# A gated SSM and MLP block: the first token tile turned by TensorE in place of a DMA transpose, and the last output piece 64 columns wide

## The chip, the cores and the metric

The kernel runs on one core of a Trainium2 chip. The metric is the device time of one execution in microseconds, as the median of several runs. Matmuls run on TensorE (PE in the profile, its weight loads are PEld), elementwise work on VectorE (DVE) and ScalarE (ACT), small set-up on GpSimd (POOL). DMAs are issued from SyncE's queue (SP) and from ScalarE's queue (ACTq).

## The reference

One input x of 2048 tokens by 640 features (bf16) goes through two branches, and a gate mixes them:

```python
g = sigmoid((x * gate_w).sum(-1, keepdims=True))
# branch A: a diagonal complex state space model with 640 states, scanned over the 2048 tokens
Lam_bar = exp(dt * Lam)
h_t = Lam_bar * h_(t-1) + B_bar @ x_t
a = 2 * real(C @ h) + x * Dskip
# branch B: an MLP, 640 -> 1728 -> 640
b = gelu(x @ w1 + b1) @ w2 + b2
out = g * a + (1 - g) * b
```

## The kernel before

**Tiling.** Tokens are worked in four chunks of 512 (CH), each of four token tiles of 128 (TPC = 4). Features are worked in five blocks of 128 (KD = 5). TensorE needs x with features on the partitions; that form is `xT[c]`, one tile of 128 x 5 x 512 for each chunk. `xn[c]` is x as it lies in memory, tokens on the partitions; branch A's skip term reads it later (`seed`, L577 to L584).

**Stages.** For each chunk: `ff1` (first MLP layer, L305), `ssm` (the B matmuls and the scan on DVE, L541), `fin_b` (second MLP layer, L606), `fin_a` (the C matmuls, the gate and the output, L654). The lines from L687 to L711 set the order of these stages by hand; the order of instructions on TensorE, DVE and ACT is the order in which the program names them, except that DVE work put off by `later` is let out by a small planner with written-down costs (`Clock`, L195). The planner's numbers are not fed by the operations that the change touches at the start.

**The start of chunk 0.** Six PSUM banks hold the first six blocks of 128 columns of the first MLP layer (FA = 6). They are filled strip by strip: strip kd is feature block kd, with weights `w1a[kd]` (128 x 768, 192 KB), and within a strip `part(kd, a)` (L356) does the six matmuls of 128 columns for token tile a. This way TensorE can begin when one token tile and one weight strip are there. Nine matmuls on a constant, up to 512 columns wide (L233), and three more (L359) run before them and have no result that is used: fillers.

How x of chunk 0 is turned:
- token tile 0, feature blocks 0 and 1 (KA = 2): by one DMA transpose straight into `xT[0]`, first on SP's queue (L140);
- token tiles 1 to 3, feature blocks 0 and 1: loaded into `xn[0]` by `load_x0` and turned by TensorE in `turn_first` (L248): two matmuls against an identity, into two PSUM tiles, then one copy to bf16 on DVE (L244) and one on ACT (L246);
- feature blocks 2 to 4 of all four tiles: loaded as `load_x0(…, KA * P, D)` and turned by `turn_rest` (L331).

The order on TensorE is: nine fillers; three fillers; part(0,0); turn_first(1); part(1,0); turn_first(2); part(0,1); part(1,1); turn_first(3); part(0,2); part(1,2); the small matmul that turns the parameters (L370); turn_rest(0); and so on.

**DMA queues.** At the head of SP's queue stand the transpose of tile 0, x of tile 2, x of tile 3, `w1a[2]`. At the head of ACT's queue stand `w1a[0]`, x of tile 1, `w1a[1]`, the rest of x for tiles 0 and 1. After them SP's queue has the parameters, the rest of x for tiles 2 and 3, the last weights strips of `w1a` (L156), `w1b` in five DMAs (L160), `w1c` in four DMAs (two strips together in the tile `w1c34`, L161, then three), the transposes of B, x and C, `w2`, and then a plain load of tile 0's first 256 features into `xn[0]` (L185), since the transpose at the head does not fill it.

Eight semaphores count the landings, in turn over both queues: each DMA takes the semaphore of the DMA eight places earlier, and its queue waits until that one has landed before it issues.

The DVE copies at L400 put one column with the gate's weights behind the 448 loaded columns of each `w1c[j]`.

**The end.** Output rows are written one token tile at a time. `cuts` (L574) says in which column pieces a tile is made: two of 320, and three for the very last tile (NT - 1). For each piece `fin_a` does ten matmuls, then DVE combines (L673). For the last tile, the first two pieces leave by one store from SP's queue (L680) and the last by a store from ACT's queue.

Of the kernel before, what the change touches and what calls it, by code (L numbers as in the profile page):

```python
# [12 lines left out]
BF16 = mybir.dt.bfloat16  # L13
# [3 lines left out]
P = 128  # L17
T = 2048
D = 640
F = 1728  # L20
CH = 512
NCH = T // CH
KD = D // P
# [3 lines left out]
NT = T // P  # L27
# [4 lines left out]
HD = D // 2  # L32
# [9 lines left out]
def kernel(  # L42
# [19 lines left out]
    nc = tc.nc  # L62
    x2d = A_x.flatten_outer_dims()
# [3 lines left out]
    const = ctx.enter_context(tc.tile_pool(name="const", bufs=1))  # L67
# [7 lines left out]
    def bank(dtype=F32):  # L75
        return ps.tile([P, CH * 4 // (4 if dtype == F32 else 2)], dtype, name="bank")
# [4 lines left out]
    cut2 = FB * P  # L81
    n1c = F - cut2 + 1
    xT = [const.tile([P, KD, CH], BF16, name=f"xT{c}") for c in range(NCH)]
# [1 line left out]
    w1a34 = const.tile([P, 2, cut1], BF16, name="w1a34")  # L85
    w1a += [w1a34[:, j, :] for j in range(2)]
    w1b = [const.tile([P, cut2 - cut1], BF16, name=f"w1b_{kd}") for kd in range(KD)]
    w1c = [const.tile([P, n1c], BF16, name=f"w1c_{kd}") for kd in range(3)]
    w1c34 = const.tile([P, 2, n1c], BF16, name="w1c34")
    w1c += [w1c34[:, j, :] for j in range(2)]  # L90
    w2_sb = const.tile([P, KF - 1, D], BF16, name="w2_sb")
    BT_re, BT_im = ([const.tile([P, KD, n * P], BF16, name=f"BT_{ri}{n}") for n in (KSA, KS - KSA)] for ri in ("re", "im"))
    CT_re = const.tile([P, KS, D], BF16, name="CT_re")
# [34 lines left out]
    def load_w1a(queue, kd):  # L128
        queue.dma_start(out=w1a[kd][:], in_=B_w1[kd * P:(kd + 1) * P, 0:cut1])  # L129
# [4 lines left out]
    KA = 2  # L134
    xn[0] = xnp.tile([P, TPC, D], BF16, name="xn")

    def load_x0(queue, a0, a1, d0, d1):
        queue.dma_start(out=xn[0][:, a0:a1, d0:d1], in_=x2d[a0 * P:a1 * P, d0:d1].rearrange("(a p) d -> p a d", p=P))  # L138

    nc.sync.dma_start_transpose(out=xT[0][:, 0:KA, 0:P], in_=x2d[0:P, 0:KA * P])  # L140
    load_w1a(nc.scalar, 0)
    load_x0(nc.scalar, 1, 2, 0, KA * P)
    load_w1a(nc.scalar, 1)
    load_x0(nc.sync, 2, 3, 0, KA * P)
    load_x0(nc.scalar, 0, H, KA * P, D)
# [12 lines left out]
    rows(nc.sync, prmB[0:KS, :], gate_w)  # L158
    for kd in range(KD):
        nc.sync.dma_start(out=w1b[kd][:], in_=B_w1[kd * P:(kd + 1) * P, cut1:cut2])  # L160
    nc.sync.dma_start(out=w1c34[:, :, 0:F - cut2], in_=B_w1[3 * P:KD * P, cut2:F].rearrange("(k p) f -> p k f", p=P))  # L161
    for kd in range(3):
        nc.sync.dma_start(out=w1c[kd][:, 0:F - cut2], in_=B_w1[kd * P:(kd + 1) * P, cut2:F])
    make_identity(nc, ident[:])
    HC = CH // 8
# [16 lines left out]
        nc.sync.dma_start(out=w2_sb[:, k0:k1, :], in_=B_w2[k0 * P:k1 * P, :].rearrange("(kf p) d -> p kf d", p=P))  # L182
    for h in range(2):
        nc.sync.dma_start(out=w2l[h * F_LAST:(h + 1) * F_LAST, :], in_=B_w2[(KF - 1) * P:F, :])
    load_x0(nc.sync, 0, 1, 0, KA * P)  # L185
    nc.sync.dma_start(out=b2bc[:], in_=B_b2.rearrange("(o d) -> o d", o=1).to_broadcast([P, D]))
    nc.sync.dma_start(out=Dbc[:], in_=A_Dskip.rearrange("(o d) -> o d", o=1).to_broadcast([P, D]))
    nc.sync.dma_start_transpose(out=xT[2][:], in_=x2d[2 * CH:3 * CH, :])
# [43 lines left out]
    pA = bank()  # L232
# [3 lines left out]
    def turn(p, col, a, kd):  # L236
        nc.tensor.matmul(p[:, col:col + P], lhsT=xn[0][:, a, kd * P:(kd + 1) * P], rhs=ident[:], start=True, stop=True,  # L237
                         skip_group_check=True)

    def turned(engine, p, col, a, k0, k1):  # L240
        dst = xT[0][:, k0:k1, a * P:(a + 1) * P]
        src = p[:, col:col + (k1 - k0) * P].rearrange("p (k t) -> p k t", t=P)
        if engine is nc.vector:
            nc.vector.tensor_copy(out=dst, in_=src)  # L244
        else:
            nc.scalar.activation(out=dst, in_=src, func=ACT.Identity)  # L246

    def turn_first(a, other):  # L248
        t = bank()
        turn(t, 0, a, 0)  # L250
        turned(nc.vector, t, 0, a, 0, 1)
        turn(other, a * P, a, 1)
        turned(nc.scalar, other, a * P, a, 1, 2)

    def col(name, dtype=F32, n=KS):
        return const.tile([P, n], dtype, name=name)
# [102 lines left out]
    for _ in range(3):  # L359
        nc.tensor.matmul(banks[0][:, 0:P], lhsT=ones(P), rhs=ones(P), start=True, stop=True, skip_group_check=True)  # L360
    part(0, 0)
    turn_first(1, pA)
    part(1, 0)
    turn_first(2, pA)
    part(0, 1)
    part(1, 1)
    turn_first(3, pA)
    part(0, 2)
    part(1, 2)
# [201 lines left out]
    HALVES = ((0, HD), (HD, D))  # L571
    seeded = {}

    def cuts(ti):  # L574
        return ((0, HD), (HD, 512), (512, D)) if ti == NT - 1 else HALVES

    def seed(ti):  # L577

        c, a = divmod(ti, TPC)
        seeded[ti] = []  # L580
        for d0, d1 in cuts(ti):
            p = bank()
            dve_now(ck.pe, 0.45, lambda: nc.vector.tensor_tensor(out=p[:, 0:d1 - d0], in0=xn[c][:, a, d0:d1], in1=Dbc[:, d0:d1], op=ALU.mult))  # L583
            seeded[ti].append(p)  # L584
# [69 lines left out]
    def fin_a(c, at={}):  # L654
        let_out(0, c)
        for a in range(TPC):
            ti = c * TPC + a
            lo = a * P
            ot = fwork.tile([P, D], BF16, name="ot", bufs=2)
            if a < TPC - 2:  # L660
                seed(ti + 2)
            if a in at:
                at[a]()
            for i, (d0, d1) in enumerate(cuts(ti)):
                p = seeded[ti][i]
                for j in range(2 * KS):
                    CT = CT_re if j < KS else CT_im
                    nc.tensor.matmul(p[:, 0:d1 - d0], lhsT=hs[c][:, j, lo:lo + P], rhs=CT[:, j % KS, d0:d1],  # L668
                                     start=False, stop=(j == 2 * KS - 1), skip_group_check=True)
                    pe(d1 - d0)  # L670

                def f():
                    nc.vector.scalar_tensor_tensor(out=ot[:, d0:d1], in0=p[:, 0:d1 - d0], scalar=gcol[:, 0, ti:ti + 1],  # L673
                                                   in1=gbs[ti][:, d0:d1], op0=ALU.mult, op1=ALU.add)

                dve_now(ck.pe + 0.2, 0.45, f)
                if ti == NT - 1 and i > 0:
                    s0 = 0 if i == 1 else d0
                    q = nc.sync if i == 1 else nc.scalar
                    q.dma_start(out=out2d[ti * P:(ti + 1) * P, s0:d1], in_=ot[:, s0:d1])  # L680
            if ti < NT - 1:
                nc.sync.dma_start(out=out2d[ti * P:(ti + 1) * P, :], in_=ot[:])
# [59 lines left out]
```

## Time and profile before

| what | us |
|---|---|
| median of 3 runs | 217.73 (217.61 to 218.08) |
| the profiled execution | 217.61 |
| its span, first to last instruction | 215.8 |
| TensorE busy | 211.0 (98%) |
| DVE busy | 188.7 (87%) |
| ACT busy | 102.7 (48%) |
| first matmul with x (L269) | at 3.92 |
| second weight strip's first matmul | at 5.47 |
| clock record of TensorE at full rate begins | at 9.16 |
| last combine on DVE begins | at 213.09 |

All times of the profile are counted from the span's start. The execution's own time is 1.81 us longer than its span. A group's count follows an x; an idle time in brackets says how long the engine sat before the group and what released it. "SPq" and "ACTq" lines are the time in which a queue issues a DMA, not the time in which its data move; landings are read from the trace's record of semaphore increments.

### The profile page before, as it was taken

To read this page: it belongs to the slowest core of one execution; us is meant where nothing else is said; L and a number is where in the kernel's file an instruction comes from. 1 tells how busy PE (TensorE), PEld (TensorE's weight loads), DVE (VectorE), ACT (ScalarE), POOL (GpSimd) and SP (SyncE) were. 2 spreads that over 40 slices of the span, in tenths; PEclk is the share of its full clock that TensorE was granted. 3 is DMA by queue.
4 is the path that set the end of the run, shared out by engine and by line. 5 is a ranking of instruction groups with operands and counts; after the bars stand their busy time and mean duration, and the time that the engine had idled before them with its cause. 6 is when DMAs were issued, how large, how long until landed. Compare 5 with 4: busy or idle time off the path is not lost.

```text
span 215.8 us, 3582 instructions
## 1 busy us (share of the span) xinstructions
PE 211.0 (98%) x1397; PEld 128.1 (59%) x1408; DVE 188.7 (87%) x386; ACT 102.7 (48%) x185; POOL 1.0 (0%) x13
## 2 busy tenths in 40 slices
PE   7999999999999999999999999999999999999994
PEld 4964544454466744675457777544456677676773
DVE  1379999999998999999999999999999999994153
ACT  3299956675668579402581310356683421404200
POOL 1000000000000000000000000000000000000000
PEclk9999999999999999999999999999999999999999
DMA  6799999994000000024000002500000000210011
GB/s 157 210 220 191 219 220 318 267 224 138 0 0 0 3 0 2 12 65 151 30 0 3 0 0 42 204 0 2 3 0 14 0 3 9 72 44 0 0 65 61
DMA packets 31843, 15.91 MB, mean 74 GB/s; under 512 B 23250, under 2 KB 31826, under 8 KB 31826
## 3 DMA queue, kind: packets, MB, share of 16 engines
q1 hardware_dynamic: 30978, 14.99, 28.2%
q10 hardware_dynamic: 848, 0.69, 1.3%
q8 instruction: 11, 0.18, 0.4%
q14 instruction: 6, 0.05, 0.1%
HBM read 7.48 MB, written 2.62 MB: 47 GB/s over the span
## 4 chain that ended last, share of the span: by engine, by line
PE 96%; DMA 2%; ACTq 0%; issue 0%; DVE 0%
PE bank L269 27%; PE bank L609 26%; PE bank L668 20%; PE bank L550 20%; DMA w1a<-in_B_w_dram 2%; PE bank L625 1%; PE bank L295 1%; PE bank L237 1%; ACTq L138 0%; ACTq L129 0%; DVE ot L673 0%; PE bank L285 0%; PE bank L370 0%; PE bank L397 0%
## 5 line engine op out<-in xcount | busy, mean ns | idle before, releaser
L609 PE MATMUL bank<-w_sb,gel 128*128 128x384 bf16 (+1 forms) x416 | 57.9, 299 | 0.0
L609 PEld LDWEIGHTS <-gel 128*128 128x128 bf16 x416 | 40.3, 98 | 17.0 <-issue 0.8
L553 ACT ACTIVATE bu<-bank 128x512 bf16<-128x512 f32 x40 | 23.6, 598 | 37.6 <-PE bank L550 37.6
L274 ACT ACTIVATE gel<-bank,colB 128x512 bf16<-128x512 f32 x52 | 33.7, 693 | 10.6 <-PE bank L269 10.4
L668 PEld LDWEIGHTS <-hs 128*128 128x128 bf16 x330 | 31.7, 98 | 11.6
L504 DVE TENSOR_TENSOR_SCAN g<-r_c,carry,v 128x512 bf16<-128x512 f32 x30 | 37.2, 1269 | 0.0
L617 ACT ACTIVATE gb<-bank,gcol 128x384 f32<-128x384 f32 (+1 forms) x32 | 15.1, 525 | 32.7 <-PE bank L609 16.4
L269 PE MATMUL bank<-xT,w1a 128*128 128x512 bf16 (+2 forms) x173 | 29.6, 328 | 0.9 <-DMA w1a<-in_B_w_dram 0.5
L668 PE MATMUL bank<-CT_re,hs 128*128 128x320 bf16 (+2 forms) x165 | 27.1, 295 | 0.0
L668 PE MATMUL bank<-CT_im,hs 128*128 128x320 bf16 (+2 forms) x165 | 27.1, 295 | 0.0
L673 DVE SCALAR_TENSOR_TENSOR ot<-bank,gcol,gb 128x320 bf16<-128x320 f32 (+2 forms) x33 | 17.4, 533 | 9.8 <-PE bank L668 9.5
L550 PE MATMUL bank<-xT,BT_im 128*128 128x512 bf16 x99 | 24.8, 379 | 0.1
L550 PE MATMUL bank<-xT,BT_re 128*128 128x512 bf16 x97 | 24.5, 379 | 0.2
L269 PEld LDWEIGHTS <-w1a 128*128 128x128 bf16 x177 | 16.2, 108 | 12.4 <-DMA w1a<-in_B_w_dram 0.8
L269 PE MATMUL bank<-xT,w1b 128*128 128x512 bf16 x80 | 17.9, 379 | 0.0
L550 PEld LDWEIGHTS <-BT_im 128*128 128x128 bf16 x100 | 9.8, 98 | 11.8
L550 PEld LDWEIGHTS <-BT_re 128*128 128x128 bf16 x100 | 9.7, 98 | 11.0
L583 DVE TENSOR_TENSOR bank<-xn,Dbc 128x320 f32<-128x320 bf16 (+2 forms) x33 | 14.5, 482 | 1.9 <-ACT gb L617 1.9
L485 DVE TENSOR_TENSOR v<-wa,wb 128x512 bf16<-128x512 bf16 x40 | 15.2, 421 | 0.6
L598 ACT ACTIVATE bank<-b2bc 128x384 f32<-128x384 bf16 (+1 forms) x24 | 11.7, 524 | 7.8 <-DVE ot L673 7.8
L485 DVE TENSOR_TENSOR wa<-TCOS,g 128x1024 bf16<-128x1024 bf16 x20 | 13.7, 685 | 0.1
L269 PE MATMUL bank<-xT,w1c 128*128 128x512 bf16 x57 | 13.6, 379 | 0.2
(99 smaller groups left out, 165.8 us busy)
## 6 DMA issues: line engine op xcount, KB each, us to landing
out_dram<-ot SPq DMA_DIRECT2D x15, 160.0 KB, 1.8
w_sb<-in_B_w_dram SPq DMA_DIRECT2D x1, 2080.0 KB
xn<-in_A_x_dram SPq DMA_DIRECT2D x3, 640.0 KB
w1b<-in_B_w_dram SPq DMA_DIRECT2D x5, 128.0 KB, 3.1
w1a<-in_B_w_dram ACTq DMA_DIRECT2D x2, 192.0 KB
w1a<-in_B_w_dram SPq DMA_DIRECT2D x1, 384.0 KB, 3.5
w1c<-in_B_w_dram SPq DMA_DIRECT2D x3, 112.0 KB, 4.3
w1c<-in_B_w_dram SPq DMA_DIRECT2D x1, 224.0 KB, 4.0
```

Source lines behind the costliest of these rows:

```text
L269: nc.tensor.matmul(p[:, t0:t1], lhsT=w, rhs=xT[c][:, kd, t0:t1], start=(kd == 0) if first is None else first, stop=(kd == last), skip_grou ...
L274: nc.scalar.activation(out=gel[c][:, kf, :], in_=p[:, :], func=ACT.Gelu_apprx_tanh, bias=b1_c[:, kf:kf + 1])
L485: nc.vector.tensor_tensor(out=o, in0=a, in1=b, op=op)
L504: nc.vector.tensor_tensor_scan(s["g"][:, ri, :], r_c[:, ks:ks + 1].to_broadcast([P, CH]), s["v"][:, ri, :], init, ALU.mult, ALU.add)
L550: nc.tensor.matmul(p[:], lhsT=BT[ks >= KSA][:, kd, (ks % KSA if ks < KSA else ks - KSA) * P:][:, 0:P], rhs=xT[c][:, kd, :], start=(kd == 0 ...
L553: nc.scalar.activation(out=bu[:, ri, :], in_=p[:], func=ACT.Identity)
L583: dve_now(ck.pe, 0.45, lambda: nc.vector.tensor_tensor(out=p[:, 0:d1 - d0], in0=xn[c][:, a, d0:d1], in1=Dbc[:, d0:d1], op=ALU.mult))
L598: nc.scalar.activation(out=v, in_=src, func=ACT.Identity)
L609: nc.tensor.matmul(p[:, col:col + d1 - d0], lhsT=gel[c][:, kf, a * P:(a + 1) * P], rhs=w2_sb[:, kf, d0:d1], start=False, stop=False, skip_ ...
L617: nc.scalar.activation(out=gbs[ti][:, d0:d1], in_=p[:, col:col + d1 - d0], func=ACT.Identity, scale=gcol[:, 1, ti:ti + 1])
L668: nc.tensor.matmul(p[:, 0:d1 - d0], lhsT=hs[c][:, j, lo:lo + P], rhs=CT[:, j % KS, d0:d1], start=False, stop=(j == 2 * KS - 1), skip_group ...
L673: nc.vector.scalar_tensor_tensor(out=ot[:, d0:d1], in0=p[:, 0:d1 - d0], scalar=gcol[:, 0, ti:ti + 1], in1=gbs[ti][:, d0:d1], op0=ALU.mult, ...
```

## The change

- The DMA transpose at the head of SP's queue becomes a plain load of the same 128 x 256 block into `xn[0]`, and the later load of the block (L185) goes.
- Tile 1's load moves from ACT's queue, where it stood between `w1a[0]` and `w1a[1]`, to SP's queue, where it comes second.
- `turn_first(0, pA)` is added: TensorE turns tile 0's two blocks between the nine fillers and the three fillers, with one copy on DVE and one on ACT.
- `w1c` is five tiles with a DMA each, in place of three and a double one.
- The last tile's pieces are 320, 256 and 64 columns in place of 320, 192 and 128.

Everything else keeps its order on TensorE, DVE and ACT.

```diff
-    w1c = [const.tile([P, n1c], BF16, name=f"w1c_{kd}") for kd in range(3)]
-    w1c34 = const.tile([P, 2, n1c], BF16, name="w1c34")
-    w1c += [w1c34[:, j, :] for j in range(2)]
+    w1c = [const.tile([P, n1c], BF16, name=f"w1c_{kd}") for kd in range(KD)]
...
-    nc.sync.dma_start_transpose(out=xT[0][:, 0:KA, 0:P], in_=x2d[0:P, 0:KA * P])
+    load_x0(nc.sync, 0, 1, 0, KA * P)
     load_w1a(nc.scalar, 0)
-    load_x0(nc.scalar, 1, 2, 0, KA * P)
+    load_x0(nc.sync, 1, 2, 0, KA * P)
     load_w1a(nc.scalar, 1)
     load_x0(nc.sync, 2, 3, 0, KA * P)
...
-    nc.sync.dma_start(out=w1c34[:, :, 0:F - cut2], in_=B_w1[3 * P:KD * P, cut2:F].rearrange("(k p) f -> p k f", p=P))
-    for kd in range(3):
+    for kd in range(KD):
         nc.sync.dma_start(out=w1c[kd][:, 0:F - cut2], in_=B_w1[kd * P:(kd + 1) * P, cut2:F])
...
-    load_x0(nc.sync, 0, 1, 0, KA * P)
...
         turned(nc.scalar, other, a * P, a, 1, 2)
 
+    turn_first(0, pA)
+
...
     def cuts(ti):
-        return ((0, HD), (HD, 512), (512, D)) if ti == NT - 1 else HALVES
+        return ((0, HD), (HD, D - P // 2), (D - P // 2, D)) if ti == NT - 1 else HALVES
```

## The prediction

> **What bounds the kernel now.** I read the page first (busy shares and the clock row), then the chain that ended last, then the timeline of the first six and last five microseconds, and last the busy time by stretch. The page:
>
> ```profile
> PE 211.0 (98%) x1397; PEld 128.1 (59%) x1408; DVE 188.7 (87%) x386; ACT 102.7 (48%) x185; POOL 1.0 (0%) x13
> ```
>
> TensorE is busy all the time, so only its first work, its pace and what follows its last matmul can move the end. The chain, in order of time:
>
> ```profile
> 1.59 0.03 issue
> 1.62 3.81 DMA w1a<-in_B_w_dram
> 5.43 0.05 issue
> 5.47 0.82 PE bank L269 x6
> ...
> 9.28 0.01 PE bank L370
> ...
> 202.16 10.91 PE bank L668 x90
> 213.06 0.03 issue
> 213.09 0.35 DVE ot L673
> ```
>
> The one transfer on it is the second weight strip, w1a_1: third DMA on ACT's queue, issued at 1.62, landed at 5.43. After 5.47 nothing but TensorE until the last `ot`. The timeline of TensorE there, and of the end:
>
> ```profile
> 3.28 0.53 PE L360 MATMUL bank<-const-bfloat16-1.0 128*128 128x128 bf16 x3
> 3.92 0.80 PE L269 MATMUL bank<-xT,w1a 128*128 128x128 bf16 x6
> 4.51 0.42 PE L237 MATMUL bank<-ident,xn 128*128 128x128 bf16 x2
> 5.47 0.82 PE L269 MATMUL bank<-xT,w1a 128*128 128x128 bf16 x6 [0.54 <-DMA w1a<-in_B_w_dram]
> ```
> ```profile
> 212.53 0.91 DVE L673 SCALAR_TENSOR_TENSOR ot<-bank,gcol,gb 128x192 bf16<-128x192 f32 x2 [0.27 <-PE bank L668]
> 212.60 0.44 PE L668 MATMUL bank<-CT_im,hs 128*128 128x128 bf16 x5
> 212.97 0.33 SPq L680 DMA_DIRECT2D out_dram<-ot  x1
> 213.47 0.36 ACTq L680 DMA_DIRECT2D out_dram<-ot  x1
> ```
>
> Two holes: 3.60 (3.495, start of the last filler, plus 0.107) to 3.92, for the DMA transpose (it lands at 3.88 by its semaphore), and 4.73 to 5.47, for w1a_1. The pace, by stretch (first to last us, length, then busy time and count on PE, PEld, DVE, ACT, POOL, clock, DMA share and GB/s):
>
> ```profile
> 5.47:9.16 3.69, 3.69 (x36) 3.69 (x37) 0.58 (x2) 0.55 (x2) 0.00 (x0) 1.00 0.68 196
> 9.16:14.00 4.84, 4.79 (x64) 4.00 (x63) 3.49 (x14) 4.06 (x9) 0.00 (x0) 1.00 0.90 251
> ```
>
> 36 matmuls of 128 columns take 3.69 us before 9.16, 0.107 apart; after it they are 0.056 apart. The clock record starts at 9.164, 3.69 us after the restart at 5.47. So what ends TensorE's last hole sets both the start and the moment of full pace.
>
> **What the skill says.** "TensorE: Matmul & The Clock Gate", Part 1: the array runs at half rate until about 3.4 us of sustained work; the window runs free, so the moment varies; starts are 107 ns apart cold and 56 ns warm at 128 columns. The trace agrees on both paces, and on one rise 3.69 us after a hole; that its moment varies no run here shows. "DMA: Bandwidth & Descriptors", "Issuing engines are not separate DMA queues": SP's and ACT's DMAs share the same 16 engines. "Queues, rings and completion order": a ring is consumed in order, and rings alternate by packet. The trace fits: x1, issued 0.48 after w1a_0 on one queue, lands 0.54 after it (3.67 against 3.13).
>
> **The start, step by step.** Removed: the transpose at SP's head (issue 1.29) and x1 between w1a_0 and w1a_1 on ACT (issue 1.14 to 1.59, with its gap 0.485). Added: a plain 64 KB load of x0 at SP's head, x1 second there; two turns on TensorE, one DVE and one ACT cast.
>
> 1. x0 lands. Nearest rows: x1 took 2.53 from issue, w1a_0 2.40. Issued at 0.73: 3.2 (2.9 if it is quicker without a ring ahead of it, 3.7 if both first issues slow each other).
> 2. Turns: the nine fillers end at 3.28. Two turns of 0.107 from 3.28 to 3.5; the three fillers (0.32) follow to 3.82. Turn to cast is 0.35 (4.515 to 4.866), the DVE cast 0.29, release 0.04: strip block 0 starts at 3.97 against 3.92, +0.05 (0 to +0.5 with a late x0). The hole before it shrinks to 0.15. ACT's new cast (0.28) comes after the table load, which moves from 2.79 to about 2.3 with one issue less; done at about 4.1, before its reader at 4.8.
> 3. The block's six matmuls (0.64) and tile 1's turns (0.21) end at 4.82. x1, issued at about 1.3 on SP, by its 2.53 lands at 3.8: in time.
> 4. w1a_1 is issued at 1.14, not 1.62. If it keeps its 3.80 it lands at 4.94 and TensorE restarts at 4.98: -0.49. If, with nothing between it and w1a_0 in its ring and no transpose beside it, it takes 3.6 or less, it is there at 4.82 and the hole is gone. Worst: the 192 KB move no faster for being asked for earlier, 5.43, gain nil. The bytes ahead of it are the same (x0 for the transpose, x1 in the other ring). I take 4.94.
> 5. With the restart 0.49 earlier and the rise still 3.69 behind it, the rise is at 8.67 and everything after shifts by 0.49. If the hole goes, the last hole ends at 3.97, the rise comes at 7.66, and the sum is larger: 34.6 cold slots ran from 5.47 to 9.16; from 4.82, 26.5 fit until 7.66, the other 8 take 8x0.056=0.45: 8.11 against 9.16, -1.05.
>
> Supply stays ahead. SP's later issues each wait for the landing eight DMAs back: x tiles 2 and 3's rest, now waiting on w1a_1, goes at 5.0 in place of 5.97, w1a's last strips at about 5.4 in place of 6.43. Their slack was 1.7 and 1.5 us (landed 8.40 and 9.96, needed at 10.10 and 11.48). Tightest is x2: needed 0.51 after the restart (5.49), issued some 0.25 earlier, so landed at about 5.4; slack 0.1 where it was 0.33. If that cover goes, the cost is the lateness itself.
>
> **w1c in five DMAs and x0's second load gone.** One issue more (0.43 on SP, median 3 rows) and one less later (0.58). w1c is needed from 18.6; its last piece landed at 15.8. B's transposes behind it had 4.6 us or more (19.0 against 23.64). The DVE copies into w1c's last columns no longer wait for that DMA: 0.33 of DVE idle at 13.8 to 14.1 goes; the weight load at 14.49 that waits on them had 0.16 of slack, so this cover gets better, and the path gets nothing. Zero.
>
> **Later slack.** Where matmuls of the output wait on DVE, the smallest margins are 1.25 (at 176.24) and 1.19 (181.68). A shift up to 1.2 reaches the end whole even if DVE did not move; DVE itself starts from TensorE's early matmul (colA at 9.35), so it moves along.
>
> **The tail.** The last tile is cut 320, 256, 64 in place of 320, 192, 128. TensorE: 10x0.0825+10x0.056=1.38 before; 256 columns are 0.109 apart (strip rows at 11.5), 65 columns 0.61/20=0.0305: 1.09+0.31=1.40, +0.01. DVE: 0.551, 0.418, 0.351 at 320, 192, 128 columns, about 1.04 ns a column: 0.485 and 0.285. The 256 piece starts at 212.79 and ends at 213.28; the 64 piece is ready at 213.10 but queues behind it, ends near 213.50 (213.44 before). ACT's store then lands 1.50 later, 215.03 against 214.97. SP's store goes at 213.30 in place of 212.97 and with its 1.72 plus 0.03 for wider rows lands at 215.05. So SP's store becomes last: +0.08 (0 to +0.2; short rows of 128 bytes are not in the trace).
>
> **Sum.** -0.49 + 0.08 = -0.41: span 215.4, and the profiled execution's 217.61 (span plus 1.81) goes to 217.2. The median shown, 217.73, is 0.12 above that execution: 217.32, say 217.3.
>
> **Rivals.**
> A. The hole at w1a_1 closes (step 4's lower end). For it: w1a_1's packets start near 3.1, after a lull, and would now follow w1a_0's at once. Against: its 16 landings spread over 1.2 us. -1.05+0.08: 216.8.
> B. Early clock: the 0.15 us hole does not count and 3.69 runs from 0.77: the rise by 4.5 to 5.8, up to -1.9, of which DVE's margin may clip some: 215.9 to 216.5. Against: 0.32 of idle was enough to prevent it before.
> C. Nothing gained: w1a_1 lands at 5.4 as before, or x0 comes at 3.7 or later so that blocks 0 and 1 follow each other with no earlier end; tail +0.08: 217.7 to 217.8.
> D. Slower: the clock. If the window runs free, the 3.69 was luck and can be up to 6.8. Each us of later rise costs 0.48 (half pace). With the restart at 4.98 half of the start's gain stays (0.52x0.49=0.25); slower by more than 0.2% needs 0.44+0.25-0.08=0.61 from the clock: a rise 1.3 later than before, past 10.4. For it: the three times spread by 0.47. Against: all three lie close above the lowest. Time 218.2 to 218.6.
>
> **Chances.** Forecast 0.38, A 0.25, B 0.07, C 0.12, D 0.18. 0.2% (0.44 us) is about what a measurement here can tell from none; the forecast stands on that edge, so I give half of it to each side: faster 0.25+0.07+0.19=0.51, same 0.19+0.12=0.31, slower 0.18. The range holds the forecast, A, C and the near half of D: 216.6 to 218.3, some 0.84. The forecast's own range is 217.1 to 217.5.
>
> **What would show it.** Restart of strip 1's block at about 4.98 (A: 4.82 with no hole; C: 5.4 or later); clock record starting at 8.7 (A 7.7, B below 6, D past 10.4); w1a_1 landing 3.8 after an issue at 1.14; block 0 at 3.97; the weight load at w1b not waiting; SP's last store landing after ACT's, some 2.2 us after the last matmul's start. Wrong it would be if x0 lands after 3.7, if the clock's rise is not tied to the last hole, or if some store or weight strip is late.

## The result and the profile after

The changed kernel takes 216.12 us (median of 6 runs, 215.99 to 216.24); the kernel before, run beside it, 217.84 (217.21 to 218.08, 6 runs). The ratio is 0.9924, 95% interval 0.991 to 0.9938. The forecast was 217.3, its range 216.6 to 218.3: the direction was right, the gain was four times the one forecast, and the time lies below the range. The profiled execution took 215.99 with a span of 214.2; before, 217.61 and 215.8.

The page's busy times after:

```profile
PE 209.9 (98%) x1399; PEld 127.1 (59%) x1410; DVE 188.9 (88%) x387; ACT 103.2 (48%) x186; POOL 1.0 (0%) x13
```

TensorE has two matmuls more and yet 1.1 us less of busy time: it ran fewer of them at half pace. The chain that ended last, in order of time (start, length, what):

```profile
0.77 2.72 PE bank L230 x9
3.49 0.21 PE bank L233 x2
3.70 0.32 PE bank L358 x3
4.02 0.75 PE bank L267 x6
4.77 0.21 PE bank L233 x2
4.99 0.64 PE bank L267 x6
...
200.31 10.62 PE bank L666 x80
210.93 0.02 issue
210.95 0.48 DVE ot L671
211.44 0.19 DVEq L735
```

No DMA is left on it. The timeline of TensorE in those microseconds:

```profile
3.28 0.42 PE L233 MATMUL bank<-ident,xn 128*128 128x128 bf16 x2
3.50 0.52 PE L358 MATMUL bank<-const-bfloat16-1.0 128*128 128x128 bf16 x3
3.97 0.80 PE L267 MATMUL bank<-xT,w1a 128*128 128x128 bf16 x6
4.57 0.42 PE L233 MATMUL bank<-ident,xn 128*128 128x128 bf16 x2
4.78 0.84 PE L267 MATMUL bank<-xT,w1a 128*128 128x128 bf16 x6
```

Block 0 starts at 3.97 and strip 1's block at 4.78, with nothing idle ahead of it: w1a_1, issued at 1.16, has landed at 4.19. The hole of 0.74 is gone. The pace, by stretch (first to last us, length, busy time and count on PE, PEld, DVE, ACT, POOL, granted clock, DMA share, GB/s):

```profile
4.00:6.00 2.00, 2.00 (x21) 2.00 (x20) 0.52 (x2) 0.41 (x3) 0.00 (x0) 1.00 0.79 232
6.00:9.00 3.00, 3.00 (x56) 2.99 (x54) 1.73 (x8) 1.39 (x6) 0.00 (x0) 1.00 0.89 272
```

21 matmuls in 2 us, then 56 in 3: the pace nearly doubles at about 6.0. The clock record begins at 6.03; before it began at 9.16. The tail (the two last DVE combines stand in one group):

```profile
210.95 0.68 DVE L671 SCALAR_TENSOR_TENSOR ot<-bank,gcol,gb 128x256 bf16<-128x256 f32 x2 [0.54 <-PE bank L666]
211.47 0.33 SPq L678 DMA_DIRECT2D out_dram<-ot  x1
211.66 0.36 ACTq L678 DMA_DIRECT2D out_dram<-ot  x1
```

**Where the 1.6 us between the two profiled executions went.** Strip 1's block starts 0.69 earlier (4.78 against 5.47). The clock: before, 34.5 matmuls of 0.107 fill the 3.69 us up to the rise at 9.16; after, 11.7 of them fit between 4.78 and 6.03 and the other 22.8 take 0.056 each, 1.28 us. The same work is done at 7.31 in place of 9.16, 1.85 earlier, of which 0.69 is the start and 1.16 the earlier rise. It arrives whole: the last tile's first combine starts 1.84 earlier (209.86 against 211.70). From there to the last landing it takes 3.52 in place of 3.26: the tail costs 0.25. Sum -1.85 + 0.25 = -1.60; the span moved by -1.59.

This settles one pair of executions. It does not say that the kernel before always rises at 9.16, nor whether it could have used an earlier rise; the runs below go into both. Nor is its start fixed: in the three other profiles with its order of loads at the start, w1a_1 landed at 5.63, 5.71 and 5.03 and strip 1's block began at 5.67, 5.76 and 5.07. The 0.69 of this pair could have been 0.29 to 0.98.

### The profile page after: what moved, and what is told of

Read it like the earlier page. It is cut to its first block, busy times and chain, and to the rows that moved or that the text cites. A ratio compares the mean times of both kernels' runs of the same rounds, so it can differ in the third digit from the quotient of the medians.

```text
span 214.2 us, 3591 instructions
## 1 busy us (share of the span) xinstructions
PE 209.9 (98%) x1399; PEld 127.1 (59%) x1410; DVE 188.9 (88%) x387; ACT 103.2 (48%) x186; POOL 1.0 (0%) x13
## 4 chain that ended last, share of the span: by engine, by line
PE 98%; issue 0%; DVE 0%; DVEq 0%
PE bank L607 27%; PE bank L267 27%; PE bank L666 20%; PE bank L548 20%; PE bank L230 1%; PE bank L623 1%; PE bank L293 1%; PE bank L233 1%; DVE ot L671 0%; PE bank L358 0%; DVEq L735 0%; PE bank L283 0%; PE bank L395 0%; PE bank L368 0%
## 5 line engine op out<-in xcount | busy, mean ns | idle before, releaser
L666 PEld LDWEIGHTS <-hs 128*128 128x128 bf16 x330 | 31.7, 98 | 11.7
L267 PE MATMUL bank<-xT,w1a 128*128 128x512 bf16 (+2 forms) x173 | 28.4, 317 | 0.2
L267 PEld LDWEIGHTS <-w1a 128*128 128x128 bf16 x177 | 15.3, 102 | 11.4
L581 DVE TENSOR_TENSOR bank<-xn,Dbc 128x320 f32<-128x320 bf16 (+2 forms) x33 | 14.5, 481 | 2.5 <-ACT gb L615 2.5
L596 ACT ACTIVATE bank<-b2bc 128x384 f32<-128x384 bf16 (+1 forms) x24 | 11.7, 526 | 7.2 <-DVE ot L671 7.2
```

The costliest lines, as they stand in the source:

```text
L267: nc.tensor.matmul(p[:, t0:t1], lhsT=w, rhs=xT[c][:, kd, t0:t1], start=(kd == 0) if first is None else first, stop=(kd == last), skip_grou ...
L596: nc.scalar.activation(out=v, in_=src, func=ACT.Identity)
```

## The experiments

Twelve runs were made, eleven of other kernels and one of the kernel before again. Times are medians, ratios are to the kernel before run beside them (its medians were 217.65, 217.56 and 217.83 in the three groups that were timed). "Rise" is the start of the clock record at full rate; each run has one profile, so a rise is known for one execution of each kernel, not for all that its median stands for.

### The order on ACT's queue alone

```diff
     load_w1a(nc.scalar, 0)
-    load_x0(nc.scalar, 1, 2, 0, KA * P)
     load_w1a(nc.scalar, 1)
+    load_x0(nc.scalar, 1, 2, 0, KA * P)
```

The kernel before, with w1a_1 ahead of x1.

> Before's kernel with one edit: on ScalarE's queue w1a_1 is issued ahead of x of tile 1, as nothing else changes (the DMA transpose stays). If the order of the queue alone made w1a_1 early, it lands by 4.3 us as in the changed kernel, the hole of TensorE ahead of strip 1's first block shrinks to 0.3 us or less and the clock record starts near 6: total about 1.5 us less than before. If the transpose beside it is what holds w1a_1 up, it lands at 4.9 or later, TensorE still has idle 0.3 + 0.4 us before 5, the clock record starts at 8.7 to 9.2, and the total falls by 0.2 to 0.5 us.

Measured: 217.45 (216.69 to 219.26), ratio 0.9997 [0.9981, 1.0014]. w1a_1 lands at 4.15, so its place in ACT's queue alone makes it early, with the DMA transpose still beside it; but x1 now lands at 5.29, TensorE restarts at 5.33, and strip 1's block begins at 5.45, no earlier than before. The odd part is the clock: it rose at 4.76, which ought to have been worth some 2 us, and the time didn't move. The waits between 9 and 17 us (who waited for what; us in total, times, longest) say where it went:

```profile
DVE w1c L400 <- DMA w1c<-in_B_w_dram: 1.8, 1, 1.8
PEld L269 <- DVE w1c L400: 1.5, 1, 1.5
PE bank L269 <- DVE w1c L400: 1.0, 1, 1.0
```

DVE's copies into the last columns of w1c wait for the joined load of w1c34; the next weight load from w1b waits for the copies; and TensorE stands for 1.0 us. This is the wait to which the prediction gave a slack of 0.16 and a value of nothing.

### x1 back on ACT's queue

```diff
     load_w1a(nc.scalar, 0)
-    load_x0(nc.sync, 1, 2, 0, KA * P)
+    load_x0(nc.scalar, 1, 2, 0, KA * P)
     load_w1a(nc.scalar, 1)
```

The kernel after, with x1 between w1a_0 and w1a_1 again.

> The changed kernel with x of tile 1 put back on ScalarE's queue between w1a_0 and w1a_1. If the transpose was what held w1a_1 up, w1a_1 is issued at 1.6 and still lands by 4.8, there is no hole beyond 0.15 us, the clock record starts near 6.0 and the time is within 0.2 us of the changed kernel's 216.1. If the order of the queue matters, w1a_1 lands at 5.0 or later, a hole of 0.3 to 0.6 us opens at 4.8, the clock record starts at 8.7 to 9.4 and the time is 217.2 to 217.6.

Measured: 216.97 (216.17 to 218.80), ratio 0.9979 [0.996, 0.9998]: 0.55% of the gain of 0.76% is lost. w1a_1, issued at 1.65, lands at 6.14, and TensorE's timeline has a hole larger than before's:

```profile
6.19 0.51 PE L267 MATMUL bank<-xT,w1a 128*128 128x128 bf16 x6 [1.18 <-DMA w1a<-in_B_w_dram]
```

So the turn on TensorE needs x1's move: without it w1a_1 is later in this profile than in any of the kernel before. The clock rose at 5.24, early in that hole (it begins at 5.01): the moment is not tied to the hole's end, and a larger hole went with an earlier rise than the first profile of before shows.

### The last piece, both ways

```diff
-        return ((0, HD), (HD, D - P // 2), (D - P // 2, D)) if ti == NT - 1 else HALVES
+        return ((0, HD), (HD, 512), (512, D)) if ti == NT - 1 else HALVES
```

The kernel after with 128 columns in its last piece:

> The changed kernel with the last tile cut 320, 192, 128 as before. If the 64-column piece costs what the two traces show (0.25 us from the last 320-column combine to the last landing), the time is 0.25 us below the changed kernel, 215.85; if it costs the predicted 0.08, 216.05; the last store's landing comes 1.5 us after its issue again, not 1.7.

And the reverse edit, the kernel before with 64 columns:

> Before's kernel with the last tile cut 320, 256, 64. The mirror of the run with the tail put back: 0.25 us slower than before by the traces, 0.08 us by the prediction. The start is untouched, so the clock record should start at 9.2 with a hole of 0.74 us ahead of strip 1's first block.

Measured: 215.41 (215.21 to 216.01), ratio 0.9895 [0.9876, 0.9915], with 128 columns on the kernel after; 217.92 (216.96 to 219.27), 1.0015 [1.0002, 1.0028], with 64 on the kernel before. The narrow piece costs 0.15% to 0.29% both ways, 0.3 to 0.6 us of median, and some 0.27 between the profiled tails (3.52 against 3.25 from the last tile's first combine to the last landing, after against this run). On the kernel after the medians differ by more than the tails do, and why stays open. The kernel after with 128 columns is below both the kernel before and the kernel after, though it was timed in four runs only.

### w1c joined again, and w1c split alone

```diff
-    w1c = [const.tile([P, n1c], BF16, name=f"w1c_{kd}") for kd in range(KD)]
+    w1c = [const.tile([P, n1c], BF16, name=f"w1c_{kd}") for kd in range(3)]
+    w1c34 = const.tile([P, 2, n1c], BF16, name="w1c34")
+    w1c += [w1c34[:, j, :] for j in range(2)]
...
-    for kd in range(KD):
+    nc.sync.dma_start(out=w1c34[:, :, 0:F - cut2], in_=B_w1[3 * P:KD * P, cut2:F].rearrange("(k p) f -> p k f", p=P))
+    for kd in range(3):
```

The kernel after with this edit:

> The changed kernel with w1c's strips 3 and 4 put back into one tile and one DMA, so that the DVE copy into its last column waits for that DMA. If the split was worth nothing (the prediction's zero), 216.1 as the changed kernel. If the joined DMA is a wall that an earlier TensorE runs into, as the trace of order_only suggests, it lands at about 12.9, the weight load that waits on the copies stands at 13.1 instead of 12.7, and the time is 0.3 to 0.7 us above the changed kernel.

The kernel before with its reverse and nothing else:

> Before's kernel with w1c split into five DMAs and nothing else. Prediction's zero: 217.6 as before. If the joined DMA is a wall, executions in which TensorE's clock rises early can now use it: 0.3 to 0.8 us less than before in the median; a profile with the rise at 9 or later would show no gain.

Measured: 216.95 (216.15 to 218.04), ratio 0.9968 [0.9954, 0.9982], joined; 216.11 (8 runs), 0.9945 [0.9918, 0.9973], split alone. The split, which the prediction priced at zero, brings 0.55% by itself, and taking it out of the kernel after costs 0.44%. The chain of the joined kernel shows how:

```profile
5.91 0.30 DVE xT L243
6.32 0.30 SPq L132
6.66 0.36 SPq L160
...
8.96 4.45 DMA w1c<-in_B_w_dram
13.43 0.24 DVE w1c L401 x2
13.71 5.35 PE bank L270 x24
```

Its clock had risen at 5.88, TensorE was at its first w1b matmul at 12.65, did one, and then stood 0.68 until 13.71. Of the five DVE copies the last two come only after the load; in the kernel after, all five go through together, 1 us before the first piece of w1c (12.71) has landed (the joined kernel first, then the kernel after):

```profile
13.43 0.23 DVE L401 CAST w1c<-bank 128x1 bf16<-128x1 f32 x2 [1.49 <-DMA w1c<-in_B_w_dram]
```
```profile
11.66 0.41 DVE L398 CAST w1c<-bank 128x1 bf16<-128x1 f32 x5
```

The column that a copy writes is not one that the load writes. In a tile of its own it has nothing to wait for; in the double tile the column of the first half lies between the columns of the one load, and the copy waits for that load, with the last copy behind it. So there is a moment, the landing of the joined load and the copies behind it, before which TensorE cannot go past its first w1b matmul; it is called the wall below.

The eight runs with w1c split alone were 215.54, 215.68, 216.03, 216.10, 216.12, 216.19, 217.80 and 217.83: six of them some 1.5 us below the kernel before, two equal to it. Two values from one program is what a clock that rises early in most executions and late in some would give; the one profile, of the 215.54, has its rise at 3.97, and no slow one was profiled. (That profile also had w1a_1 at 5.03, 0.40 before the kernel before's, ahead of anything that the split touches; the median does not rest on it.)

### The three fillers behind the turn, and five of the nine ahead of it

```diff
-    for n in (512, 512, 512, 512, 512, 128, 128, 128, 128):
+    for n in (512, 512, 512, 512):
...
-    for _ in range(3):
-        nc.tensor.matmul(banks[0][:, 0:P], lhsT=ones(P), rhs=ones(P), start=True, stop=True, skip_group_check=True)
```

The first of these two runs makes only the second edit, the other makes both; both on the kernel after.

> The changed kernel without the three fillers between tile 0's turns and the first block: TensorE is idle 0.47 us before 3.97 in place of 0.15. If the clock rises at the end of a free-running window that may be idle for about a quarter (0.85 us), nothing changes: clock record starting between 3.4 and 6.8, time within 0.2 us of the changed kernel. If a hole over some 0.2 us restarts the count, the record starts at 7.4 or later and the time is 0.7 to 1.2 us above the changed kernel.

> The changed kernel with four fillers of 512 columns alone: idle from 2.48 to 3.28 and from 3.49 to 3.97, 1.27 us in all, with the same data at the same times. If a window may be idle for a quarter, none that holds both holes passes, so the clock record starts between 6.3 and 9.7, and the time is 0.7 to 1.5 us above the changed kernel. If only the last restart counts, it is as with no mid fillers.

Measured: 215.86 (215.18 to 216.27), ratio 0.9924 [0.9908, 0.994], rise at 3.75, without the three; 216.77 (216.36 to 217.39), 0.9969 [0.9958, 0.9979], rise at 7.68, with four fillers in all. Block 0 starts within 0.03 of 3.97 in both. Fillers that keep TensorE busy ahead of 3.3 are worth 0.45%; since block 0 starts no earlier for them, what is left for it is the clock; the three behind the turn are worth nothing that can be measured, with a hole of 0.48 in their place.

### The missing corner: joined w1c and a late clock

The kernel with w1c joined and with the four fillers alone (both edits above).

> The kernel after with w1c joined again and with only the four wide fillers: the corner that is missing between 'kernel after', 'w1c joined' (216.95) and 'four fillers' (216.77). Theory (the joined w1c load is a wall that stands at about 13.4 to 13.7 us, so it costs only where the clock has risen early): with four fillers the weight load of w1b comes at 13.2 in place of 12.4, the wall costs TensorE 0 to 0.2, so 216.8 to 217.0, ratio to before 0.997 to 0.998, near that of four fillers. Rival (splitting w1c is worth a constant amount, from the queue or from DVE): the 0.8 us that joining costs under nine fillers is paid again, 217.5 to 217.6, ratio 1.000 to 1.001.

Measured: 217.12 (216.36 to 217.65), ratio 0.9966 [0.9953, 0.9979]. With the other three runs this makes a square, all with the kernel after's order at the start:

| ratio to before | w1c joined | w1c in five |
|---|---|---|
| nine and three fillers (rises at 5.88 and 6.03) | 0.9968 | 0.9924 |
| four fillers (rises at 9.26 and 7.68) | 0.9966 | 0.9969 |

Splitting w1c is worth 0.44% where the clock rises early and nothing where it rises late. An early clock is worth 0.45% with w1c split and nothing with it joined. Within the intervals, some 0.13% to each side, neither has a value of its own; each pays only where the other is there. (In the joined kernel with four fillers the joined load landed at 13.08 and TensorE came to its first w1b matmul at 14.1, so it never met the wall.)

### The split with the order, and the best combination

```diff
     load_w1a(nc.scalar, 0)
-    load_x0(nc.scalar, 1, 2, 0, KA * P)
     load_w1a(nc.scalar, 1)
+    load_x0(nc.scalar, 1, 2, 0, KA * P)
...
-    for kd in range(3):
+    for kd in range(KD):
```

The kernel before with w1c in five tiles and w1a_1 ahead of x1; what is left to the 128-column kernel after is the turn of tile 0 with x1 on SP's queue.

> The kernel before with w1c in five DMAs and w1a_1 issued ahead of x1 on ACT's queue; the DMA transpose of tile 0 and the last piece of 128 columns stay. It is the kernel after with 128 columns at the end, less the turn of tile 0 on TensorE. Theory: order alone was worth 0.0 and the split alone 0.55%; with the wall gone the start's 0.1 to 0.2 us (strip 1's block at 5.33 with the holes of the run with order alone, against 5.47) can be kept: ratio 0.993 to 0.995, about 216.1 to 216.4; the turn on TensorE is then worth the rest to the 0.9895 of the run with 128 columns, some 0.9 us. Rival: the turn adds nothing, ratio 0.989 to 0.991, about 215.4. A second rival: the two holes of 0.6 and 0.26 keep the clock low in more executions: 0.997 or above.

Measured: 216.16 (215.88 to 217.29), ratio 0.9936 [0.9911, 0.9962]. The order adds nothing that can be told from the split alone (0.9945); the turn with x1 on SP is, by difference, the other 0.4% on the way to 0.9895. TensorE's timeline shows what it takes away:

```profile
4.22 0.49 PE L266 MATMUL bank<-xT,w1a 128*128 128x128 bf16 x6 [0.41 <-DMA xT<-in_A_x_dram]
5.32 0.28 PE L234 MATMUL bank<-ident,xn 128*128 128x128 bf16 x2 [0.60 <-DMA xn<-in_A_x_dram]
5.44 0.50 PE L266 MATMUL bank<-xT,w1a 128*128 128x128 bf16 x6
```

With the transpose at SP's head and x1 third on ACT's queue, strip 1's block starts at 5.44; in the kernel after it starts at 4.78, because both x0 and x1 go first on SP's queue and both weight strips first on ACT's.

The kernel after with 128 columns at the end and without the three fillers:

> The kernel after without the three fillers between the turn of tile 0 and its block, and with 128 columns in the last piece. Theory: the three fillers do nothing for the start (0.9924 with and without them) and the last piece's 64 columns cost 0.3%: ratio 0.989 to 0.990, 215.3 to 215.6, the best with the run that changes the last piece alone. Rival: a hole of 0.47 ahead of the first block makes the clock rise later in more executions than the 64 columns had let show: 0.991 to 0.993.

Measured: 215.69 (215.02 to 215.91), ratio 0.990 [0.988, 0.9921]. It cannot be told from the kernel with 128 columns alone (0.9895). About 215.5, 1% below the kernel before, is what these parts give.

### The kernel before, profiled once more

> The kernel before, unchanged, with a second profile: does the clock's rise come at the same moment of the same program? Theory (the window that decides the clock runs free of the kernel, and one with up to about a quarter of idle still passes): the clock record begins somewhere in 3.4 to 5.5 or in 8.7 to 10.3, not at 9.16 again; if it begins early, TensorE runs into the joined w1c load and waits 0.7 or more on the DVE copies into w1c between 12 and 14.5, and the time stays within 0.6 of 217.7. Rival (the rise is tied to the end of the last hole at 5.47, as the prediction's fifth step has it): 9.1 to 9.3, and no wait of TensorE on w1c.

Measured: 217.41 (one run, 217.87 for the other of the same kernel beside it). The same program's clock rose at 4.49 in place of 9.16, and 4.7 us of full pace were worth 0.2 us. The waits between 9 and 17 us, where the first profile of this kernel has none of TensorE on w1c:

```profile
DVE w1c L400 <- DMA w1c<-in_B_w_dram: 1.9, 1, 1.9
PEld L269 <- DVE w1c L400: 1.6, 1, 1.6
PE bank L269 <- DVE w1c L400: 1.1, 1, 1.1
```

And its chain:

```profile
1.62 4.01 DMA w1a<-in_B_w_dram
5.67 0.51 PE bank L269 x6
6.29 0.67 PE bank L269 x12
7.06 0.30 DVE xT L244
7.36 0.19 SPq L132
...
9.76 0.43 SPq L160
10.24 3.98 DMA w1c<-in_B_w_dram
14.24 0.24 DVE w1c L400 x2
14.53 5.35 PE bank L269 x24
```

TensorE reached its first w1b matmul at 13.02, did one, and went on at 14.53. With the clock rising at 9.16, the first profile's TensorE comes to the same place at 14.49, when its copies have hardly waited:

```profile
14.11 0.23 DVE L400 CAST w1c<-bank 128x1 bf16<-128x1 f32 x2 [0.33 <-DMA w1c<-in_B_w_dram]
```

Both executions pass this place at 14.5, one matmul apart, with clocks 4.7 us apart. The slack of 0.16 which the prediction read there meant this: TensorE, with a late clock, comes to the wall just as it opens, and with an early one it stands and waits for it.

## Why the prediction was wrong, step by step

Two steps failed: the tie of the clock's rise to the last hole (step 5), and the zero for w1c in five DMAs. In the two profiled executions the start gave -0.69 in place of -0.49, the rise another -1.16 in place of nothing, and the tail +0.25 in place of +0.08. The earlier rise reached the end whole because w1c was split: with w1c joined and the clock as early, TensorE's second w1b matmul starts at 13.71, in the kernel after at 12.87, so that 0.84 of it would have been lost.

**Steps 1 to 3 (x0, the turns, x1): right.** x0 landed at 3.17 (3.2 said), block 0 started at 3.97 (3.97), x1 landed at 3.94 (3.8) ahead of its turn at 4.57.

**Step 4 (w1a_1): the lower end came true.** It took 3.02 from issue, not 3.80, and landed at 4.19; 3.6 or less was named as what closes the hole, as in rival A. The run with the order alone had it at 4.15 beside the DMA transpose, so the transpose alone was not what had slowed it; with x1 back in between it took 4.49 and landed at 6.14. The start is worth 0.69 in place of 0.49 from this alone.

**Step 5 (the rise is 3.69 behind the last hole): failed.** The rise came 1.25 behind strip 1's block and 2.06 behind block 0, past a 0.15 hole. Rival B's argument against itself, that 0.32 of idle had been enough to prevent an early clock, falls as well: the same program with the same kind of holes rose at 4.49. The Trainium skill, "TensorE: Matmul & The Clock Gate", Part 1, has the clock decided by windows of 3413 ns that run free of the kernel, and the runs agree: all 14 records of full clock last 208.21 or 211.63 us before their first break, 61 and 62 times 3.4133. The same part puts the rise about 4 us into sustained work, "±500ns run-to-run"; here it comes 2.96 to 8.87 us after the first filler (at 3.73 to 9.64), so that does not hold in these runs. A reading that fits all of them is that a window decides by how much of it TensorE was busy, with a good part of idle allowed. The two windows that lie closest to the line are these, the one that ended in the rise of the kernel with the order alone, and the one that would have had to pass for the kernel before's first profile to rise at 5.75:

```profile
1.34:4.76 3.42, 2.78 (x16) 1.54 (x14) 0.10 (x1) 1.49 (x2) 0.26 (x7) 1.00 0.73 189
```
```profile
2.34:5.75 3.41, 2.76 (x20) 1.97 (x19) 0.29 (x1) 1.76 (x3) 0.00 (x0) 1.00 0.93 254
```

The first is of the order-only kernel and raised the clock with 2.78 busy on PE, the second is of the kernel before and did not with 2.76. In the other runs, those that raised it have 2.9 to 3.4, and those that did not 2.5 or less. A share near 0.81 divides all of them, but by 0.02 us and by a view whose matmul ends are modelled. Counted by starts instead, with 0.107 for each 128 columns, the two windows hold 2.57 and 2.35, and the fullest that did not raise the clock 2.43 (the kernel with 128 columns, -0.22 to 3.20): the order is the same, the share is then between 0.71 and 0.75. So the size of the share depends on how busy time is counted, and that it is a share of a window was inferred from these profiles and not tried by itself. With it, before's holes (1.06 of idle together by the starts, 0.65 by the view) leave it to the window's phase whether the rise comes early or one window later. The kernel after has no hole from 3.97 on, so by this reading a window fails only for what lies before its fillers' start; it and its five variants with nine fillers rose between 3.75 and 6.61.

**"w1c in five DMAs": failed, and the step that lost the most.** The text had the right wait, the right instructions and the right slack, and concluded "the path gets nothing. Zero." It measured -0.55% alone and -0.44% within the change, about 1 us. For an execution with a late clock zero is about right: with four fillers the split is worth nothing that can be measured. The mistake was to price the wait (the weight load of w1b on the copies into w1c, with 0.16 of slack) from one execution, whose TensorE was late, while the same text held that the rise can vary (rivals B and D) and quoted the skill for it. Had rival B been worked through to the w1b weight load, 1.9 us earlier would have been set against a cover of 0.16, and both the kernel before's insensitivity to the clock and the worth of the split would have come out of it.

**Supply and later slack: right.** x2 landed at 4.48, ahead of its turn at 5.42. SP's queue moved earlier (its first w1c load was issued at 9.01, w1c34 at 10.06 before), since its issues wait on earlier landings. This also moved the wall: with w1c joined again TensorE goes on at 13.71, in place of 14.53. That would explain why the new start is worth about as much with the wall (0.9968 against 1.0015 of the kernel before, both with 64 columns: 0.47%) as without it (0.9895 against 0.9945, both with 128: 0.50%; each difference is uncertain by 0.2 to 0.35). TensorE's lead of 1.84 reached the last tile whole.

**The tail: right step, one term mis-sized.** Taken into the frame of the kernel before (plus 1.84), the 256 piece starts at 212.79 (212.79 said), SP's store goes at 213.31 (213.30) and lands at 215.06 (215.05). ACT's store was said to land 1.50 after its issue, at 215.03; it took 1.72 and landed at 215.22, after SP's. That is +0.25 in place of +0.08. In seven profiles with 64 columns it takes 1.71 to 1.76, in seven with 128 columns 1.47 to 1.51. The stores are then 0.20 apart in place of 0.50 and the rows 128 bytes long in place of 256; which of the two it is was not tried.

**Rivals.** A had the start right and its time (216.8) wrong, since it kept the rise tied to the hole and knew no wall. B came nearest. Its clock was early, as measured (4.5 to 5.8 said, 6.03 in the profile), and its time, 215.9 to 216.5, holds the median; all six profiles of kernels with the new turn and nine fillers rose before 7, so its chance of 0.07 was too small. That is in part luck: its count of 3.69 from the first filler is not what the runs show, and like the forecast it priced the split at nothing, without which its early clock would have ended at the wall. D's mechanism, a free window, fits the runs; its sign was wrong, since the kernel before gained nothing from an early rise and so had no luck to lose.

**A misreading.** x1 was issued 0.41 behind w1a_0 in the kernel before (0.73 and 1.14), not 0.48; no sum rests on it.

**The whole.** In percent of the median the change comes out as -0.5 for the start, -0.5 for the split and +0.15 to +0.3 for the tail: -0.7 to -0.85, against -0.76 measured.

## What to carry to other kernels

A slack read from one execution holds for that execution's pace alone: before a wait is priced at nothing, shift its reader by everything else that the change brings, and ask again. Where a bound engine's start depends on luck (here the clock), look for the next wall behind it: the kernel before took the same time to 0.2 us with its clock 4.7 us earlier, and the chain of its first profile did not show what held it. Write a tile's own columns apart from what a joined load spans, or the writer waits for the load.

## What had not been expected of the hardware

- The clock's rise fell at 4.49 and 9.16 in two profiles of one program, and some idle did not prevent it: in the kernel with the order alone it rose at 4.76 with TensorE idle, by the view, for 0.64 of the 3.42 us before. With x1 back on ACT's queue it stayed up through the rest of a hole of 1.18 within which it had risen (5.24).
- w1a_1, a weight strip of 192 KB, took 2.88 to 4.49 us from issue, by what stood next to it: 2.88 to 3.19 right behind the first strip on ACT's queue (nine profiles), with the transpose or with the x loads on SP's; 3.41 to 4.10 behind x1 on ACT with the transpose on SP (four profiles); 4.49 behind x1 on ACT with plain loads on SP (one).
- ACT's last store lands 1.71 to 1.76 after its issue with rows of 64 columns, 1.47 to 1.51 with 128.
